# Counting a smaller, growing delay between last byte and use for the first twelve transfers, in the list that orders the first block

## The chip, the cores and the metric

The kernel runs on one core of one Trainium2 chip. The metric is the device time of one execution in microseconds (us); lower is better. The engines are called as in the profile: PE (TensorE matmuls), PEld (TensorE weight loads), DVE (VectorE), ACT (ScalarE), POOL (GpSimd), SP (SyncE, which here issues every DMA; SPq is its queue).

## What is computed

A windowed attention (4 batches, 8 heads, 576 positions, head width 64; heads 0 to 3 look back 32 positions, heads 4 to 7 look back 128 in steps of 4), then two feed-forward layers over 2304 tokens of width 512 with 2048 hidden units:

```python
scores = np.where(masks, scale * np.matmul(q, k.transpose(0, 1, 3, 2)), -1e9)
attn = softmax(scores)                      # rows
x = np.matmul(attn, v)                      # -> (2304, 512)
h = x @ w_in                                # layer 1, rational activation
P = a[0] + a[1] * h + a[2] * h**2 + a[3] * h**3
Q = 1.0 + np.abs(b[0]) * np.abs(h) + np.abs(b[1]) * h**2
x = (P / (Q + 1e-06)) @ w_out
h = x @ w2_in                               # layer 2, PReLU
out = (np.maximum(h, 0.0) + alpha * np.minimum(h, 0.0)) @ w2_out
```

The softmax is written out here as one call; the reference subtracts the row maximum, takes the exponential and divides by the sum plus 1e-9. All arrays are float32; the layer-1 weights come in as 64-bit words, from which a float32 is rebuilt on the chip (`w_convert`).

## The kernel before

The 2304 tokens are cut into six blocks of 384 (`BLK`). The attention of a block is four units U (pairs of heads); units 0 to 3 are block 0, units 4 to 7 block 1. One unit goes through these steps: its qk and v tiles are loaded (`u_load`, L439 and L441); PE writes the mask into PSUM (`put`, L458) and adds the scores on top (L478); DVE takes the row maxima `mx` (L492) and scales them to `nm` (L496); ACT takes the exponentials `p` with their sums `sm` (L512); DVE inverts the sums to `rd` (L522, L523), and either DVE (L541, units 0 to 3) or ACT (L532, later units) normalises `p`; PE transposes it (L549); ACT (L568) and DVE (L570) copy the transposes to `pts`; PE multiplies by v (L582, the "PV" below); ACT copies the result to `xh` (L609), and from block 1 on DVE takes the remainder `xl` (L615).

Layer 1 then runs in pairs of hidden chunks. For a chunk c ("item") PE does eight matmul instructions of `xh` with the rebuilt weights `win` (L645, two a matmul in block 0), into one of two PSUM banks `ps_h`; ACT makes `ta` (L663) and `tc` (L664) from it; DVE works on `tc` (L665, L666), and L666 is the last reader of the bank; the pair's rest (`rat_2`) alternates DVE L672, ACT L673 and L674, DVE L675 to L677. The second matmuls (L695, `outproj1`) accumulate into `ps_y`. The weights of a chunk pair are rebuilt by two ACT copies (L375, first `raw_inh`, then `raw_outh`) and DVE steps (L381, two L391, two L396). In the trace the first weight tiles are `win_342`, `win_418`, `wout_495` and `win_503`, in this order; the number is the tile's.

All loads go through SP's queue in the order of the string `ORDER` at the start: mask constants, qk of unit 0, identity, qk of unit 1, two small tables, v of unit 0, qk of unit 2, and so on, then weights. Ten `warm` matmuls (L963, 128x512 bf16) and 64 `fill` matmuls (L967, 128x256 bf16) compute nothing that is used.

The order of instructions on PE, DVE, ACT and SP is not the order in which the code writes them. `in_order_of_need` collects all instructions, derives which needs which, gives each a level (the longest chain behind it), and then runs a list schedule in an assumed time: on the engine that is free first it takes the instruction with the highest level among those that are ready within `SLACK` (100 ns). What starts before `ORDERED` (115 us of the assumed time) is fixed in this order on its engine; all the rest keeps the code's order behind it. Nothing is timed on the chip for this: costs come from `_cost`, and the landing of a transfer from these lines (L245 to L248):

```python
            parts, width = size[k]
            begin = max(start + 1600, landed)
            landed = begin + parts * width / (412 if parts == 128 else 210)
            done = landed + (2700 if begin > start + 1700 else 900)
```

So the list lets one transfer's bytes follow the other's at 412 bytes a ns, and counts another 900 ns (transfer alone) or 2700 ns (it had to queue behind an earlier one) from its last byte to the moment at which an engine may use it. The real semaphores decide on the chip; the list only decides who stands before whom on each engine, and an engine runs its instructions in that order.

Of the kernel before, what the change touches and what calls it, by code (L numbers as in the profile page):

```python
# [29 lines left out]
FILLS = (64,)  # L30
W_BIAS = 2.0 ** -112
NARROW = 2.1
SLACK = 100.0
FILL = 256
ORDERED = 115e3
# [65 lines left out]
def _cost(i):  # L101
# [22 lines left out]
    if e == mybir.EngineType.Activation:  # L124
        far = outs and any(abs(s) != 1 for s, _ in outs[0].ap[-1:]) and outs[0].dtype == F32R
        acc = len(outs) > 1
        occ = max(165, (1.7 if far else NARROW if outs[0].dtype == mybir.dt.uint16 else 0.95) * n) + 93 * pointers + 50 * acc
        return occ, occ + 145 + (12 if acc else 0)
# [7 lines left out]
def in_order_of_need(tc, nc, places):  # L136
# [88 lines left out]
            waiting[todo[k].engine].append(k)  # L225
    order = {e: [] for e in free}
    landed = 0.0
    for _ in range(n):
        pick = None
        for e, w in waiting.items():  # L230
            if not w:
                continue
            t = min(max(free[e], ready_at[k]) for k in w)
            if pick is None or t < pick[0]:
                pick = t, e
        t, e = pick
        limit = max(t, free[e]) + SLACK
        k = max((k for k in waiting[e] if ready_at[k] <= limit), key=lambda k: level[k])
        waiting[e].remove(k)
        start = max(free[e], ready_at[k])  # L240
        if start < ORDERED:
            order[e].append(k)
        free[e] = start + costs[k][0]
        if e == Engine.SP:
            parts, width = size[k]  # L245
            begin = max(start + 1600, landed)
            landed = begin + parts * width / (412 if parts == 128 else 210)
            done = landed + (2700 if begin > start + 1700 else 900)  # L248
        else:
            done = start + costs[k][1]  # L250
        for j, data in after[k]:
            left[j] -= 1
            ready_at[j] = max(ready_at[j], done if data else free[e])
            if not left[j]:
                waiting[todo[j].engine].append(j)
# [11 lines left out]
def attn_rational_prelu_kernel(  # L267
# [853 lines left out]
    rest()  # L1121
    out_some(len(todo))
    in_order_of_need(tc, nc, slots)


# [80 lines left out]
```

## Time and profile before

| what | value |
|---|---|
| time, median of 3 runs | 888.12 us (887.09, 888.12, 888.78) |
| the profiled execution: time, span | 887.51 us, 885.7 us |
| PE busy | 872.5 us, 99% of the span |
| DVE busy | 760.7 us, 86% |
| ACT busy | 613.3 us, 69% |
| DMA | 92.78 MB, mean 105 GB/s; 328 GB/s over the first 60 us |
| instructions | 14822 |

The profiled execution is one more run than the three. Its span runs from the first to the last recorded instruction; the 1.8 us by which its time is longer lie around it. Busy shares are means over stages; which engine holds up the end in a stage is read from a window or a chain of that stage.

### The profile page before, as it was taken

The numbers are of one execution on the slowest core, as the hardware profiler recorded it, in microseconds if no ns is written. First come the engines' busy times: TensorE is split into PE (matmuls) and PEld (weight loads), VectorE is DVE, ScalarE is ACT, GpSimd is POOL, SyncE is SP. The second block draws the span as 40 slices with busy tenths as digits, with TensorE's granted clock in tenths as the row PEclk, the third lists the DMA queues.
The fourth block names the chain that finished last, engine by engine and source line by source line (L and its number), as shares of the span: only waits on it lengthen the run. The fifth ranks groups of instructions, "written<-read, shape, count | busy, mean of one in ns | idle before, by whom it ended". The sixth has DMA issues, their size and how long they took to land.

```text
span 885.7 us, 14822 instructions
## 1 busy us (share of the span) xinstructions
PE 872.5 (99%) x5746; PEld 779.0 (88%) x5746; DVE 760.7 (86%) x1199; ACT 613.3 (69%) x1253; POOL 0.2 (0%) x4
## 2 busy tenths in 40 slices
PE   9999999999999999999999999999999999999997
PEld 6555678999999999999999999898888989899896
DVE  5999999999999998988899999998986778767652
ACT  6999988788877888887677576557554456635423
POOL 0000000000000000000000000000000000000000
PEclk9999999999999999999999999999999999999999
DMA  9964212133334434440021242323320011210001
GB/s 346 407 238 176 82 57 79 38 115 140 130 109 139 173 125 148 160 149 19 20 78 42 95 131 95 119 79 119 101 85 24 27 46 60 97 47 25 1 0 72
DMA packets 32903, 92.78 MB, mean 105 GB/s; under 512 B 3905, under 2 KB 11329, under 8 KB 32833
## 3 DMA queue, kind: packets, MB, share of 16 engines
q1 hardware_dynamic: 32832, 91.83, 29.9%
q8 instruction: 45, 0.74, 0.3%
q14 instruction: 26, 0.20, 0.1%
HBM read 76.61 MB, written 15.20 MB: 104 GB/s over the span
## 4 chain that ended last, share of the span: by engine, by line
PE 57%; ACT 18%; DVE 18%; DMA 4%; issue 2%; SPq 0%; ACTq 0%
PE ps_h L836 19%; PE ps_y L714 14%; PE ps_y L695 9%; PE ps_h L645 7%; PE ps_aS L714 4%; PE ps_aP L714 3%; ACT p L512 3%; DVE tb L675 2%; DVE tc L676 2%; ACT p L532 2%; ACT tc L664 2%; ACT ta L673 2%; DVE tc L677 2%; ACT ta L674 2%; ACT ta L663 1%
## 5 line engine op out<-in xcount | busy, mean ns | idle before, releaser
L645 PE MATMUL ps_h<-xh,winh 128*128 128x384 f32 x320 | 110.4, 345 | 2.7 <-DVE tc L666 2.2
L695 PE MATMUL ps_y<-gh,wouth 128*128 128x384 f32 x320 | 108.4, 339 | 0.0
L695 PE MATMUL ps_y<-gl,wouth 128*128 128x384 f32 x320 | 107.1, 335 | 0.3 <-DVE gl L685 0.3
L695 PE MATMUL ps_y<-gh,woutl 128*128 128x384 f32 x320 | 107.2, 335 | 0.0
L645 PE MATMUL ps_h<-xh,winl 128*128 128x384 f32 x320 | 107.2, 335 | 0.0
L645 PE MATMUL ps_h<-xl,winh 128*128 128x384 f32 x320 | 107.1, 335 | 0.0
L714 PE MATMUL ps_y<-wouth,gl 128*128 128x512 f32 x192 | 74.9, 390 | 0.0
L714 PE MATMUL ps_y<-woutl,gh 128*128 128x512 f32 x192 | 74.9, 390 | 0.0
L714 PE MATMUL ps_y<-wouth,gh 128*128 128x512 f32 x192 | 74.8, 390 | 0.0
L663 ACT ACTIVATE ta<-ps_h,root 128x384 f32<-128x384 f32 x96 | 57.3, 596 | 18.7 <-PE ps_h L645 18.4
L664 ACT ACTIVATE tc<-ps_h,co 128x384 f32<-128x384 f32 x96 | 66.5, 694 | 0.0
L645 PEld LDWEIGHTS ps_h<-xh,winh 128*128 128x128 f32 x320 | 60.0, 188 | 6.9 <-DVE tc L666 3.7
L742 ACT ACTIVATE gh<-tc 128x768 fp32r<-128x768 f32 x48 | 40.3, 841 | 30.5 <-PE ps_aP L714 28.0
L695 PEld LDWEIGHTS ps_y<-gl,wouth 128*128 128x128 f32 x320 | 60.2, 188 | 0.6 <-DVE gl L685 0.6
L645 PEld LDWEIGHTS ps_h<-xl,winh 128*128 128x128 f32 x320 | 60.1, 188 | 0.3
L743 DVE TENSOR_TENSOR gl<-tc,gh 128x768 fp32r<-128x768 f32 x48 | 45.8, 954 | 16.9 <-ACT gh L742 16.7
L695 PEld LDWEIGHTS ps_y<-gh,wouth 128*128 128x128 f32 x320 | 60.2, 188 | 0.0
L742 ACT ACTIVATE st_a<-w 128x1024 fp32r<-128x1024 f32 x24 | 25.5, 1061 | 50.1 <-PE ps_h L836 41.4
L695 PEld LDWEIGHTS ps_y<-gh,woutl 128*128 128x128 f32 x320 | 60.1, 188 | 0.0
L645 PEld LDWEIGHTS ps_h<-xh,winl 128*128 128x128 f32 x320 | 60.1, 188 | 0.0
L675 DVE SCALAR_TENSOR_TENSOR tb<-tb,ta 128x768 f32<-128x768 f32 x48 | 45.8, 955 | 16.3 <-ACT ta L674 16.0
L666 DVE SCALAR_TENSOR_TENSOR tc<-tc,co,ps_h 128x384 f32<-128x384 f32 x96 | 58.1, 608 | 0.7
(197 smaller groups left out, 2317.8 us busy)
## 6 DMA issues: line engine op xcount, KB each, us to landing
w<-w_dram_in SPq DMA_DIRECT2D x24, 512.0 KB, 3.6
raw<-in_w_in_dram SPq DMA_DIRECT2D x16, 512.0 KB, 5.1
raw_inh<-in_w_out_dram SPq DMA_DIRECT2D x13, 512.0 KB, 3.8
ld_qk<-in_qk_d_dram SPq DMA_DIRECT2D x12, 512.0 KB, 5.0
ld_v<-in_v_d_dram SPq DMA_DIRECT2D x12, 512.0 KB, 4.1
ld_qk<-in_qk_p_dram SPq DMA_DIRECT2D x12, 416.0 KB, 4.2
ld_v<-in_v_p_dram SPq DMA_DIRECT2D x12, 384.0 KB, 3.4
y_dram<-os SPq DMA_DIRECT2D x24, 192.0 KB, 1.9
```

The costliest lines, as they stand in the source:

```text
L512: nc.scalar.activation(out=a["p"][h][:m, t * n:(t + 1) * n], in_=a["s"][h][:m, t * n:(t + 1) * n], func=AF.Exp, scale=scale, bias=a["nm"][ ...
L532: nc.scalar.activation(out=pv, in_=pv, func=AF.Copy, scale=rd[:m, t:t + 1])
L645: nc.tensor.matmul(out=hp[:, :BLK], lhsT=w, rhs=x, start=(k == 0), stop=(k == len(pairs) - 1))
L663: nc.scalar.activation(out=ta, in_=hp, func=AF.Abs, scale=root)
L664: nc.scalar.activation(out=tc_, in_=hp, func=AF.Identity, scale=co[:, 3:4], bias=co[:, 2:3])
L666: nc.vector.scalar_tensor_tensor(out=tc_, in0=tc_, scalar=co[:, 1:2], in1=hp, op0=ALU.add, op1=ALU.mult)
L675: nc.vector.scalar_tensor_tensor(out=tb, in0=tb, scalar=C1, in1=ta, op0=ALU.add, op1=ALU.mult)
L695: nc.tensor.matmul(out=yt[:, :BLK], lhsT=w[:, m * 128:(m + 1) * 128], rhs=g, start=(c == 0 and i == 0), stop=(c == NC - 1 and i == len(pai ...
L714: nc.tensor.matmul(out=yt, lhsT=g[:, tok], rhs=w, start=(first and i == 0), stop=(last and i == 2))
L742: nc.scalar.activation(out=hi, in_=t, func=AF.Copy)
L743: nc.vector.tensor_tensor(out=lo, in0=t, in1=hi.bitcast(F32), op=ALU.subtract)
L836: nc.tensor.matmul(out=hp, lhsT=u[:, ws], rhs=x[:, xs], start=(k == 0), stop=(k == 5))
```

## The change

```diff
+LAG = 2700
...
     order = {e: [] for e in free}
     landed = 0.0
+    issued = []
...
             begin = max(start + 1600, landed)
             landed = begin + parts * width / (412 if parts == 128 else 210)
-            done = landed + (2700 if begin > start + 1700 else 900)
+            done = landed + (min(LAG, 300 + 450 * len(issued)) if begin > start + 1700 or len(issued) < 12 else 900)
+            issued.append(k)
```

The delay from last byte to use is now 300, 750, 1200, 1650, 2100 and 2550 ns for the first six transfers, then 2700 ns up to the twelfth whether they queue or not; from the thirteenth on it is as before (2700 for one that queued, 900 for one alone). Nothing is added to the program or taken from it: the instructions are the same, and only their order moves. The three new lines also move the line numbers: below L248 every line of the changed kernel is 3 higher (L512 is L515, L967 is L970).

In PE's order the start of the program changes. Of the rows of before, this is the piece from the end of unit 0's scores (`ps_y_251`, `ps_y_252`) to the first score of unit 1 (`ps_aS`); the pair of L967 rows stands 22 times there, and ten warm-ups stand before it:

```order
L478 MATMUL ps_y_252<-ld_qk 64x96
L458 LDWEIGHTS msk
L458 MATMUL ps_y_351<-msk 64x320
L967 LDWEIGHTS msk
L967 MATMUL ps_h<-msk 128x256
...
L478 MATMUL ps_aS<-ld_qk 64x96
```

The same place in the change, where seven warm-ups stand before the masks, two between masks and unit 0's scores, and one after these; the pair of L970 rows stands 12 times:

```order
L481 MATMUL ps_y_252<-ld_qk 64x96
L966 LDWEIGHTS warm
L966 MATMUL ps_h<-warm 128x512
L970 LDWEIGHTS msk
L970 MATMUL ps_h<-msk 128x256
...
L481 MATMUL ps_aS<-ld_qk 64x96
```

Ten fills that stood ahead of unit 1's scores now stand later: between the first two transposes and unit 2's scores, and around unit 3's.

On ACT the rows from the end of unit 0's part to the first weight copies, before:

```order
L988 ACTIVATE root<-root 128x1
L609 ACTIVATE xh_416<-ps_h 128x384
L512 ACTIVATE p,sm<-ps_y_350,nm 112x80 x4
L512 ACTIVATE p,sm<-ps_y_351,nm 112x80 x4
L512 ACTIVATE p,sm<-ps_y_426,nm 112x80 x4
L512 ACTIVATE p,sm<-ps_y_427,nm 112x80
L568 ACTIVATE pts<-ps_aS 96x384
L512 ACTIVATE p,sm<-ps_y_427,nm 112x80 x3
L375 ACTIVATE win_342<-raw_inh_150 128x512
```

and in the change:

```order
L991 ACTIVATE root<-root 128x1
L571 ACTIVATE pts<-ps_aS 96x384
L612 ACTIVATE xh_416<-ps_h 128x384
L515 ACTIVATE p,sm<-ps_y_350,nm 112x80 x4
L515 ACTIVATE p,sm<-ps_y_351,nm 112x80 x4
L515 ACTIVATE p,sm<-ps_y_426,nm 112x80 x4
L515 ACTIVATE p,sm<-ps_y_427,nm 112x80 x4
L378 ACTIVATE win_342<-raw_inh_150 128x512
```

The copy of unit 1's transposes (`pts<-ps_aS`) moved from the exponentials of unit 3 to before those of unit 2 (`ps_y_350`, `ps_y_351`).

Further on ACT, from the copies of `wout_495` over unit 4's exponentials (`ps_aS`, `ps_aP`) to the first rational steps, before:

```order
L375 ACTIVATE wout_495<-raw_inh_158 128x512
L375 ACTIVATE wout_495<-raw_outh_160 128x512
L609 ACTIVATE xh_580<-ps_h 128x2x4x48
L375 ACTIVATE win_503<-raw_inh_166 128x512
L512 ACTIVATE p,sm<-ps_aS,nm 128x96 x3
L512 ACTIVATE p,sm<-ps_aP,nm 128x96 x3
L663 ACTIVATE ta<-ps_h,root 128x384
L664 ACTIVATE tc<-ps_h,co 128x384
```

and in the change:

```order
L378 ACTIVATE wout_495<-raw_inh_158 128x512
L612 ACTIVATE xh_580<-ps_h 128x2x4x48
L378 ACTIVATE wout_495<-raw_outh_160 128x512
L666 ACTIVATE ta<-ps_h,root 128x384
L515 ACTIVATE p,sm<-ps_aS,nm 128x96 x3
L515 ACTIVATE p,sm<-ps_aP,nm 128x96 x3
L667 ACTIVATE tc<-ps_h,co 128x384
...
L676 ACTIVATE ta<-tb,c1t 128x768
L378 ACTIVATE win_503<-raw_inh_166 128x512
```

The first `ta` now stands ahead of unit 4's exponentials, and the copy of `win_503` moved from ahead of them to behind the first L676 (L673 before).

## Rows read from the trace of the kernel before

**Rows 1.** The page: its first line, and busy time (share of the span) of PE.

```profile
span 885.7 us, 14822 instructions
...
PE 872.5 (99%) x5746; PEld 779.0 (88%) x5746; DVE 760.7 (86%) x1199; ACT 613.3 (69%) x1253; POOL 0.2 (0%) x4
```

**Rows 2.** Windows: start:end, length, busy (x instructions) by engine, PEclk, DMA share, GB/s.

```profile
26.20:36.00 9.80, 8.17 (x55) 4.60 (x51) 9.39 (x20) 8.72 (x29) 0.00 (x0) 1.00 1.03 405
36.00:48.30 12.30, 11.67 (x57) 6.33 (x58) 11.70 (x22) 12.30 (x31) 0.00 (x0) 1.00 1.03 408
...
54.30:127.00 72.70, 72.08 (x463) 45.74 (x463) 71.78 (x118) 71.74 (x152) 0.00 (x0) 1.00 0.33 117
127.00:883.00 756.00, 750.73 (x4778) 701.46 (x4778) 646.15 (x987) 496.46 (x958) 0.00 (x0) 1.00 0.26 85
```

**Rows 3.** Timeline, first 9 us, PE and PEld: start, us, engine, line, out<-in, [idle before].

```profile
1.72 0.15 PEld L963 LDWEIGHTS <-warm 128*128 128x128 bf16 x1 [0.28 <-issue]
...
4.28 0.37 PEld L963 LDWEIGHTS <-warm 128*128 128x128 bf16 x2 [0.28 <-issue]
...
6.11 2.30 PEld L967 LDWEIGHTS <-msk 128*128 128x128 bf16 x22 [0.15 <-issue]
...
8.62 0.29 PE L478 MATMUL ps_aS<-ld_qk 64*64 64x96 f32 x1
```

**Rows 4.** Unit 1's qk: its issue (timeline of SP), and from the DMA view, us to landing.

```profile
2.11 0.43 SPq L439 DMA_DIRECT2D ld_qk<-in_qk_p_dram  x1
...
ld_qk<-in_qk_p_dram SPq DMA_DIRECT2D x1, 416.0 KB, 4.7
```

**Rows 5.** Timeline of DVE: scaled maxima of units 1 and 4, last reader of the second bank.

```profile
10.25 0.17 DVE L496 TENSOR_SCALAR nm<-mx 128x6 f32<-128x6 f32 x1
...
27.65 0.16 DVE L496 TENSOR_SCALAR nm<-mx 128x6 f32<-128x6 f32 x1
...
35.25 0.61 DVE L666 SCALAR_TENSOR_TENSOR tc<-tc,co,ps_h 128x384 f32<-128x384 f32 x1
```

**Rows 6.** Timeline of ACT, 10 to 50 us.

```profile
10.52 0.34 ACT L512 ACTIVATE p<-ps_aS,nm 128x96 f32<-128x96 f32 x1 [1.04 <-DVE ba L986]
...
14.68 0.33 ACT L512 ACTIVATE p<-ps_y,nm 112x80 f32<-112x80 f32 x1
...
18.81 0.49 ACT L568 ACTIVATE pts<-ps_aS 96x384 f32<-96x384 f32 x1
...
25.30 0.91 ACT L609 ACTIVATE xh<-ps_h 128x384 f32<-128x384 f32 x1
26.30 0.67 ACT L375 ACTIVATE win<-raw_inh 128x512 f32<-128x512 f32 x1
27.91 0.34 ACT L512 ACTIVATE p<-ps_aS,nm 128x96 f32<-128x96 f32 x1 [0.93 <-DVE nm L496]
...
29.82 0.61 ACT L663 ACTIVATE ta<-ps_h,root 128x384 f32<-128x384 f32 x1
...
35.72 0.84 ACT L674 ACTIVATE ta<-ta 128x768 f32<-128x768 f32 x1
...
47.81 1.72 ACT L532 ACTIVATE p<-p,rd 128x96 f32<-128x96 f32 x6
```

**Rows 7.** Timeline of PE, 24 to 49 us.

```profile
24.72 0.88 PE L645 MATMUL ps_h<-xh,win 128*128 128x384 f32 x2 [0.16 <-DVE win L396]
...
26.19 4.78 PE L645 MATMUL ps_h<-xh,win 128*128 128x384 f32 x14
...
35.92 2.20 PE L645 MATMUL ps_h<-xh,win 128*128 128x384 f32 x6 [0.64 <-DVE tc L666]
...
48.26 0.31 PE L549 MATMUL ps_aS<-ident,p 128*96 128x128 f32 x1 [0.30 <-ACT p L532]
```

**Rows 8.** Waits, 100 to 150 us, PE's own: in total, times, longest.

```profile
PE ps_h L582 <- ACT wouth L416: 0.4, 1, 0.4
...
PE ps_h L645 <- DVE tc L666: 0.2, 1, 0.2
```

## The prediction

> **What bounds the kernel now.** Start with the busy times. PE is busy 872.5 of 885.7 us [rows 1], so 13.2 us are all that any reordering could take away. The windows by stage say where they lie [rows 2]. From 127 to 883 us PE is busy 750.73 of 756.00: this lies behind nearly all that the list fixes, and PE sets its pace. From 54.3 to 127 PE, DVE and ACT are busy 72.08, 71.78 and 71.74 of 72.70: three engines are full at once, so a lead of one of them alone is worth nothing there. Only before 48.3 does PE stand still for long: 1.63 us between 26.2 and 36, 0.63 between 36 and 48.3, where ACT has none left (12.30 of 12.30). The question is thus how much earlier PE comes through the first 54 us, and whether ACT and DVE come along. The granted clock reads 1.00 in all these stretches.
>
> **The start.** The timeline shows the cost of a pessimistic list: between unit 0's scores and unit 1's stand 22 fills, 2.30 us, 0.105 us each, and unit 1's scores begin at 8.62 [rows 3]. Their qk was issued at 2.11 and landed 4.7 us later, at 6.8 [rows 4]. The old list adds 2700 ns to that transfer's last byte, the new one, for the fourth transfer, 300 + 3 x 450 = 1650; the difference, 1.05 us, is ten fills of 0.105. All else ahead of unit 1's scores is the same set of instructions in another order, so they begin at 8.62 - 1.05 = 7.6. That is still 0.8 after the landing: no wait takes the place of the fills. The ten fills return later, where PE waits for DVE and ACT anyway; if that cover were gone they would cost 1.05.
>
> On DVE unit 1's `nm` now stands directly behind the maxima instead of behind one small operation on `sm` (0.1 us). So it comes from 10.25 [rows 5] to about 9.1, and unit 1's exponentials come from 10.52 [rows 6] to 9.4: a lead of 1.1 to 1.2.
>
> Unit 2 keeps part of it. Its maxima now stand on DVE in front of the copy of `ps_aP`, but its `nm` behind that copy, which waits for unit 1's transposes; by the order of steps its exponentials start at about 14.3 instead of 14.68 [rows 6], 0.4 earlier. ACT's copy of `ps_aS` (0.49 with its tail, about 0.4 of ACT's time, at 18.81 before) is done ahead of them now, which brings the lead back to 0.7 or 0.8 when unit 3's exponentials end. From there to the first L645 the three orders are nearly alike, so I carry 0.7: PE's first matmul of item 0 starts at 24.0 instead of 24.72 [rows 7]. That it is not the full 1.05 is a choice between ends, 0.4 (what unit 2's start keeps) and 1.05 (unit 1's lead); the copy decides for the upper half.
>
> **What ACT gives back.** After the weights of `wout_495` the old order gives ACT the copy of `win_503` at 26.30, then unit 4's exponentials at 27.91, held 0.93 by DVE's `nm` at 27.65 [rows 5, 6]. The new order gives it `ta` of item 0 next. Item 0 needs eight of the sixteen L645 instructions, 4.78/14 = 0.34 each, with unit 4's scores between them (from 25.60, where the first two end, to 26.19 before) [rows 7]: 24.0 + 8 x 0.34 + 0.6 = 27.3 or 27.4. ACT is done with its part at about 25.3 (the L609 that began at 25.30 no longer stands last and all is 0.7 earlier), so it stands 2.1 us, against 9.80 - 8.72 = 1.08 before [rows 2]. DVE's `nm` of unit 4 now has two L391 in front instead of one; DVE's lead pays for that one and no more, so it lies at 27.7 to 28.0. Unit 4's exponentials then start at about 28.2, end 27.91 to 29.82 = 1.91 later, at 30.1 [rows 6], and the same steps as before up to L674, `win_503` among them, end at 36.6; before it was 35.72 + 0.84 = 36.56 with the tail. ACT's lead is gone: between 0.2 behind and 0.2 ahead.
>
> PE keeps its lead a little longer. DVE reaches L666 of item 1, the last reader of the second bank, without its short waits for ACT, at some 34.9 instead of 35.86 [rows 5], so item 2's matmuls start at 35.1 instead of 35.92 [rows 7], 0.8 ahead. But ACT is full from there on, with the same work to do, and unit 5's normalising steps (47.81 before [rows 6]) start when they did. PE already waited for them at 48.26, 0.30 [rows 7]; now it arrives 0.5 to 0.6 earlier, takes two instructions of L695 forward and then waits for ACT. So about 0.5 of the 0.7 is late next at unit 5's transposes, and 0.2 stays.
>
> **Behind 54 us.** The list swaps more rows up to 115 us of its time: layer-1 work of items 2 and 3 ahead of weight copies on ACT, six matmuls of a later chunk into the front of one PE stretch, transposes of one unit split over two places. No row prices these. A gain is bounded by the waits that PE has there, 0.4 + 0.2 [rows 8]; a loss by the nearest wait for a DVE reader, 0.64 [rows 7]. I take nothing, as all three engines are full on either side, and keep both ends. SP issues the same loads; three late ones change places.
>
> **Sum.** -0.7 at item 0, +0.5 at unit 5, 0 behind: -0.2 us, against the profiled execution's 887.51 (885.7 of span and 1.8 around it): 887.3. That execution lies 0.6 below the median 888.12, inside the spread of the three runs (1.7); a new median may fall in between, so I take 887.8 as the base and predict 887.6. Bounds of the sum: -0.7 - 0.6 = -1.3 and +0.3 + 0.6 = +0.9. About 0.2% (1.8 us) is what a measurement of this kernel can tell from no change: below 886.0 is faster, above 889.6 slower.
>
> **Rivals.**
> *The lead is kept and grows.* If ACT's standing at 25 to 27 is shorter than I reckon, item 2 and 3's steps, now ahead of weight copies, feed PE in time, and PE's idle time between 26.2 and 48.3 (2.26 us [rows 2]) shrinks as well. For it: the old list was wrong by 1 us just where PE did useless work. Against it: ACT is full from 36 us on. The lead alone gives 887.1, with all the idle time 884.8; the middle is 885.9. It decides if unit 5's normalising begins by 47.2.
>
> *ACT becomes late.* The copy of `win_503` moves from 26.30 to about 34.9. If ACT stands 2.1 instead of 1.08 and the lead doesn't cover it, that 1.07 shows at items 4 and 5, whose weights these are, and again at unit 5's transposes, 2.1 in all: 889.9, slower. For it: 36 to 48.3 has no idle ACT to absorb it. Against it: DVE's lead at L666. It decides once the first `win_503` copy starts after 35.9.
>
> *The clock rises later.* The loads of the warm-ups come every 0.43 us from 1.72 on and only the two at 4.28 within 0.37 together [rows 3], which is 512 columns at 1.2 and then 2.4 GHz. In the change sixteen short mask matmuls stand where the eighth warm-up did. If the lower level lasts over the twelve fills, they cost 12 x 0.105 = 1.26 more, unit 1 is 0.2 later than before, and what ACT loses (1.07 as above) is not covered: 1.3 later, 889.1. [...] PE has work without a break in both orders, so I give it little.
>
> *The change does nothing that counts*, since all that moves is hidden: 887.8, within the forecast.
>
> **How the numbers follow.** Forecast with "does nothing": 0.56, around 887.6, own range 886.5 to 888.7, the bounds of the sum. Lead kept 0.24; ACT late 0.14; clock 0.06. Faster: most of the second, 0.19, and 0.03 of the forecast's tail, 0.22. Slower: 0.10 of ACT late and 0.02 of tail, 0.12. Same: 0.66. The range 885.3 to 889.8 leaves out the lower part of "lead kept" (0.08) and the upper of "ACT late" (0.08).
>
> **What would show it.** Right, if the profile of the change has: twelve fills before unit 1's scores, which begin near 7.6; the first L645 near 24.0; ACT idle about 2 us before the first `ta`; item 2 near 35.1; unit 5's first transpose waiting for L532 at 48.3; equal times from there. Wrong, if L532 of unit 5 starts a microsecond earlier or later than 47.81, or if PE gets new waits between 54 and 130 us.

## The result: 892.3 us, slower by 0.5%

The change runs in 892.34 us (median of 11 runs, 890.43 to 896.96); the kernel before, beside it, in 887.70 (11 runs, 886.42 to 890.92). The ratio is 1.0052, with a 95% interval of 1.0038 to 1.0066. The prediction, 887.6 with 889.8 as its upper end, was wrong.

**The profile after.** The profiled execution took 891.03 us. From the page, its first line and the busy times, the lines that answer to [rows 1]:

```profile
span 889.3 us, 14819 instructions
...
PE 874.5 (98%) x5745; PEld 779.0 (88%) x5746; DVE 760.9 (86%) x1199; ACT 613.9 (69%) x1253; POOL 0.2 (0%) x4
```

The windows of [rows 2], with the same columns:

```profile
26.20:36.00 9.80, 7.86 (x67) 4.39 (x66) 9.35 (x19) 7.40 (x26) 0.00 (x0) 1.00 1.02 404
36.00:48.30 12.30, 11.87 (x71) 6.74 (x66) 10.34 (x19) 12.30 (x31) 0.00 (x0) 1.00 1.03 409
54.30:127.00 72.70, 71.47 (x417) 44.54 (x415) 71.87 (x118) 72.27 (x152) 0.00 (x0) 1.00 0.33 117
127.00:883.00 756.00, 751.78 (x4819) 701.78 (x4820) 647.98 (x989) 496.16 (x956) 0.00 (x0) 1.00 0.25 84
```

Between 26.2 and 36 ACT does 1.32 us less than before (7.40, not 8.72), and then it is full to 48.3; from 54.3 to 127 PE does 0.61 less.

The start, from the timelines of PE and of its weight loads, for [rows 3]:

```profile
4.41 0.51 PEld L461 LDWEIGHTS <-msk 64*64 64x64 bf16 x16 [0.84 <-issue]
5.31 0.13 PEld L966 LDWEIGHTS <-warm 128*128 128x128 bf16 x2 [0.38 <-issue]
...
6.18 0.73 PE L481 MATMUL ps_y<-ld_qk 64*64 64x96 f32 x24
7.07 1.47 PE L970 MATMUL ps_h<-msk 128*128 128x256 bf16 x12 [0.16 <-issue]
8.47 0.29 PE L481 MATMUL ps_aS<-ld_qk 64*64 64x96 f32 x1
```

Twelve fills stand there, as foretold. But unit 0's scores begin at 6.18, not at 5.36 as before:

```profile
5.36 0.70 PE L478 MATMUL ps_y<-ld_qk 64*64 64x96 f32 x21
```

So unit 1's begin at 8.47, a mere 0.15 earlier than 8.62.

DVE around unit 4's scaled maxima, for the second line of [rows 5]:

```profile
27.03 0.68 DVE L394 SCALAR_TENSOR_TENSOR win<-raw_inh,win 128x512 uint32<-128x512 uint32 x1
27.63 0.45 DVE L495 TENSOR_REDUCE mx<-ps_aS 128x3 f32<-128x288 f32 x1
...
28.36 0.68 DVE L394 SCALAR_TENSOR_TENSOR win<-raw_outh,win 128x512 uint32<-128x512 uint32 x1
28.96 0.17 DVE L499 TENSOR_SCALAR nm<-mx 128x6 f32<-128x6 f32 x1
```

ACT, for [rows 6]: exponentials of units 1 and 2, the last copy of `wout_495`, the first `ta`, unit 4's exponentials, the first copy of `win_503`, unit 5's normalising steps:

```profile
10.37 0.34 ACT L515 ACTIVATE p<-ps_aS,nm 128x96 f32<-128x96 f32 x1
...
15.41 0.32 ACT L515 ACTIVATE p<-ps_y,nm 112x80 f32<-112x80 f32 x1
...
25.71 0.67 ACT L378 ACTIVATE wout<-raw_outh 128x512 f32<-128x512 f32 x1
28.75 0.58 ACT L666 ACTIVATE ta<-ps_h,root 128x384 f32<-128x384 f32 x1 [2.36 <-PE ps_h L648]
29.22 0.34 ACT L515 ACTIVATE p<-ps_aS,nm 128x96 f32<-128x96 f32 x1
...
36.06 0.66 ACT L378 ACTIVATE win<-raw_inh 128x512 f32<-128x512 f32 x1
...
49.18 1.75 ACT L535 ACTIVATE p<-p,rd 128x96 f32<-128x96 f32 x6
```

And PE, for [rows 7]: item 0, unit 4's first score among it, unit 4's transposes, item 2, unit 5's transposes:

```profile
25.04 1.53 PE L648 MATMUL ps_h<-xh,win 128*128 128x384 f32 x4 [0.16 <-DVE win L399]
26.49 0.29 PE L481 MATMUL ps_aS<-ld_qk 64*64 64x96 f32 x1
...
33.18 0.84 PE L552 MATMUL ps_aS<-ident,p 128*96 128x128 f32 x3 [1.89 <-ACT p L535]
...
36.48 2.85 PE L648 MATMUL ps_h<-xh,win 128*128 128x384 f32 x8
...
49.67 0.57 PE L552 MATMUL ps_aS<-ident,p 128*96 128x128 f32 x2 [0.40 <-ACT p L535]
```

Four matmuls of item 0 stand ahead of unit 4's scores, not two; these come at 26.49 (25.53 before). DVE does a first weight step before the maxima can begin and a second ahead of `nm`, which comes at 28.96 (27.65 before). ACT meanwhile waits 2.36 us for `ps_h`, with `ta` first in its queue. Unit 4's exponentials start 1.31 later than before, and PE waits 1.89 for their end instead of 0.93. Unit 5's normalising steps are 1.37 late.

PE's waits between 54 and 200 us, for [rows 8]:

```profile
PE ps_h L648 <- DVE tc L669: 0.7, 1, 0.7
PE ps_h L585 <- DVE tc L669: 0.7, 1, 0.7
PE ps_h L585 <- issue: 0.4, 1, 0.4
PE ps_aS L552 <- ACT p L535: 0.2, 1, 0.2
```

Before there were three waits in this stretch, the two of [rows 8] and this one: 0.9 us then, 2.0 now.

```profile
PE ps_y L695 <- DVE gl L685: 0.3, 1, 0.3
```

### The profile page after: what moved, and what is told of

Its sections match the earlier page's. It is cut to its first block, busy times and chain, and to the rows that moved or that the text cites. A ratio compares the mean times of both kernels' runs of the same rounds, so it can differ in the third digit from the quotient of the medians.

```text
span 889.3 us, 14819 instructions
## 1 busy us (share of the span) xinstructions
PE 874.5 (98%) x5745; PEld 779.0 (88%) x5746; DVE 760.9 (86%) x1199; ACT 613.9 (69%) x1253; POOL 0.2 (0%) x4
## 4 chain that ended last, share of the span: by engine, by line
PE 56%; DVE 21%; ACT 19%; issue 2%; DMA 1%; SPq 0%; ACTq 0%
PE ps_h L839 19%; PE ps_y L717 14%; PE ps_y L698 7%; PE ps_h L648 6%; PE ps_aS L717 4%; PE ps_aP L717 3%; ACT p L515 3%; DVE tc L679 3%; DVE tb L678 3%; ACT p L535 2%; ACT ta L676 2%; DVE tc L680 2%; ACT tc L667 2%; ACT ta L677 2%; ACT ta L666 2%
## 5 line engine op out<-in xcount | busy, mean ns | idle before, releaser
L717 PE MATMUL ps_y<-wouth,gh 128*128 128x512 f32 x192 | 74.8, 390 | 0.0
L745 ACT ACTIVATE st_a<-w 128x1024 fp32r<-128x1024 f32 x24 | 25.5, 1062 | 50.1 <-PE ps_h L839 41.4
```

The costliest lines, as they stand in the source:

```text
L717: nc.tensor.matmul(out=yt, lhsT=g[:, tok], rhs=w, start=(first and i == 0), stop=(last and i == 2))
L745: nc.scalar.activation(out=hi, in_=t, func=AF.Copy)
```

## The experiments

In most kernels the list is worked out twice, with the old delays (0) and the new (1), and every engine's order is put together from pieces of the two, cut by the old list's times in ns. Each piece holds whatever the old list starts in it. The core, as a diff against the kernel before (the first four kernels write the same with two pieces, `head` and `tail`):

```diff
+    lists = listed(False), listed(True)
+    at = {k: start for ks in lists[0].values() for k, start in ks}
+    order = {e: [] for e in lists[0]}
+    low = -1
+    for which, high in PIECES:
+        for e in order:
+            order[e] += [k for k, start in lists[which][e] if low <= at[k] < high and start < ORDERED]
+        low = high
```

Line numbers in these kernels are 8 to 25 higher than in the kernel before.

**Four cuts: the start, and 50 us.** The first has the new order only up to unit 0's scores, the second only behind them; the third up to 50 us, the fourth only behind it.

```diff
# e1_start_new
+CUT = 5340.0
+    head, tail = (new, old)
# e2_start_old
+CUT = 5340.0
+    head, tail = (old, new)
# e3_new_to_50
+CUT = 50e3
+    head, tail = (new, old)
# e4_old_to_50
+CUT = 50e3
+    head, tail = (old, new)
```

> Only the first 26 matmuls and unit 0's scores (what the old list starts before 5.34 us) stand in the new order, that is seven warm-ups, sixteen masks, two warm-ups, the scores, one warm-up; all behind is in the old order. Clock theory (the masks among the warm-ups let the array's lower level last longer): unit 0's scores begin at about 6.2 instead of 5.36, the 22 fills follow, unit 1's scores at about 9.4, and the time is 0.5 to 1 us above 887.7. Order theory (the clock has no part; what costs is the order behind the start): scores of unit 0 near 5.2, time 887.7 within 0.5.

> The complement: start in the old order (ten warm-ups, masks, unit 0's scores), all behind in the new order. Clock theory: unit 0's scores at 5.36 and unit 1's near 7.6, the first L645 near 24.0, and most of the 4.6 us of the change comes back: 887.5 to 889. Order theory: unit 1 is early as well, but unit 4's exponentials still wait behind the first ta and the swaps behind 54 us still cost, so the time stays at 890.5 to 892.5.

> New order for all that the old list starts before 50 us, old order behind it. If the loss comes from the first 50 us alone and the rest of it grows out of PE being 1 us late in a stage where three engines are full: 891 to 892. If the new order behind 50 us has its own price: PE is 1.0 late at 54 us as in the change, and the time is 888.5 to 889.

> Old order before 50 us, new order behind. If the loss comes from the first 50 us: 887.7 within 0.5. If the new order behind 50 us has its own price: everything is as before up to 54 us, and the time is 2 to 3 us above, 890 to 891.

Measured: e1 0.9997 (0.9987 to 1.0008), e2 1.0036 (1.0022 to 1.0049), e3 1.0026 (1.0012 to 1.0040), e4 1.0011 (0.9998 to 1.0024). The start alone costs nothing, though unit 5's first PV product is 0.68 us late in its profile (55.14, not 54.46). The stretch from 5 to 50 us costs most; of the order behind 50 us the interval allows nothing to 2 us.

Times counted from a profile's start carry chance. Unit 0's scores begin at 5.28 to 6.03 us in the eleven profiles of this document whose start has the old order, and at 5.53 to 6.28 in the nine with the new one (means 5.66 and 6.07). The profile before, with 5.36, is an early one. What is late by half a us in one profile is compared more safely from one event of a profile to another of the same profile.

**Finer pieces.** New between 5.3 and 25.5 us, new between 25.5 and 50, all new but that stretch, new between 50 and 85.

```diff
# e5_new_5_25
+PIECES = ((0, 5340), (1, 25500), (0, 1e9))
# e6_new_25_50
+PIECES = ((0, 25500), (1, 50e3), (0, 1e9))
# e7_old_25_50
+PIECES = ((1, 25500), (0, 50e3), (1, 1e9))
# e8_new_50_85
+PIECES = ((0, 50e3), (1, 85e3), (0, 1e9))
```

> The old order up to 5.3 us of the old list's times and from 25.5 us on; between them the new one: twelve fills ahead of unit 1's scores, unit 2's nm behind the copy. Theory A (what is lost lies in ACT's order from 25 to 50 us): the lead of unit 1's scores, 0.7 us in the run with the old start, is gone when item 0 begins, near 24.7, and nothing is late behind it: 888.3 to 888.8 beside 888.6, ratio 0.9997 to 1.0003, unit 5's normalising steps at 47.8 to 48.0. Theory B (unit 2's nm behind the copy is what costs, since DVE and ACT are late from there on): ratio 1.002 to 1.003, normalising steps after 48.8. If the lead is kept it is faster, 0.999.

> Only the stretch from 25.5 to 50 us of the old list's times in the new order: ACT's first ta of item 0 stands ahead of unit 4's exponentials, and the first copy of win_503 behind ta of item 1's second half. Theory A: all of the middle's loss is here; unit 4's exponentials start 1.0 to 1.3 later than 27.91, unit 5's normalising steps at 48.8 to 49.2, ratio 1.0020 to 1.0028 (1.8 to 2.5 us). Theory B: nothing is late, ratio 1.000 to 1.0007, normalising steps at 47.8 to 48.1.

> The whole of the new order but for the stretch from 25.5 to 50 us, which has the old one. Theory A: only the tail's loss is left, 1.0 us as in the run with the old order up to 50 us: ratio 1.0008 to 1.0015, unit 5's normalising steps at 48.1 to 48.4. Theory B: as the whole change, 1.003 to 1.005. If the loss in the middle and the one of the tail aren't a sum, it may come out below 1.0008.

> The old order up to 50 us of the old list's times and behind 85; between them the new one: a unit's transposes split by output matmuls, masks in another order, DVE's steps of layer 1 shuffled against each other. If the tail's 1.0 us comes from these rows (theory C), ratio 1.0008 to 1.0015, with PE waits for DVE near 103 and 126 us, and first stores of a block 1 to 1.5 later than 135.8, 215.9, 294.6. If it comes from the rows behind 85 (theory D), ratio 0.9995 to 1.0005 and none of these.

Measured: e5 1.0028 (1.0010 to 1.0046), e6 1.0019 (1.0006 to 1.0032), e7 1.0038 (1.0021 to 1.0055), e8 0.9994 (0.9982 to 1.0006). Neither theory holds by itself. With theory A, e7 should have come to 1.0015 at most; with theory B, e6 should have been nothing. Two profiles, of e6 and e7, showed one reason why the parts need not add up: the granted clock reads 0.50, the 1.2 GHz level, for some seven us behind PE's wait at unit 4's transposes. The profiles of before and of the change showed nothing of the kind.

**ACT's rows alone, the order behind 85 us, and a cover for the wait.** f1 moves eleven rows of ACT and nothing on other engines; f2 takes ACT's rows back in the change; f3 is new behind 85 us only; f4 is the change with twelve small matmuls in PE's wait.

```diff
# f1_act_alone (the pieces hold for ACT; 0 on the other engines)
+PIECES = ((0, 25500), (1, 36000), (0, 1e9))
...
# f2_act_back (the pieces hold for ACT; 1 on the other engines)
+PIECES = ((1, 25500), (0, 36000), (1, 1e9))
...
# f3_new_behind_85
+PIECES = ((0, 85e3), (1, 1e9))
# f4_cover (other lines set these matmuls directly ahead of unit 4's transposes in PE's order)
...
+            if not J:
+                cover = bank("y0")
+                for _ in range(12):
+                    nc.tensor.matmul(out=cover[:, :COVER], lhsT=ident16, rhs=msk[:, :COVER], start=True, stop=True)
```

> The kernel before with eleven rows of ACT alone in the new order (25.5 to 36 us of the old list's times): first ta ahead of unit 4's exponentials, the first copy of win_503 behind the last of them; PE, DVE and SP keep the old order row by row. Theory A (this order is the middle's loss): unit 4's exponentials start 1.0 to 1.5 later than 27.91, PE waits 1.5 to 1.9 ahead of unit 4's transposes, unit 5's normalising steps at 48.6 to 49.2; ratio 1.0018 to 1.0026, as the run with this stretch new on all engines. Rival (the loss came from PE's and DVE's rows of that stretch): ratio within 1.0005 of 1.

> The changed kernel with these rows of ACT alone (25.5 to 36 us) back in the old order. Theory A: the middle's loss of about 2 us goes, what is left is that of the other stretches, 1.0 to 1.6: ratio 1.0012 to 1.0030 instead of 1.0052, unit 5's normalising steps a microsecond earlier than 49.18. Rival: 1.0045 to 1.0055 as the whole change.

> The old order up to 85 us of the old list's times, the new one behind. The new order behind 50 us cost 1.0, the piece from 50 to 85 alone gained 0.5 or nothing; so by a sum this one costs 1.0 to 1.5: ratio 1.0010 to 1.0018, with a PE wait for a DVE reader near 180 us where the change splits the transposes. Rival (the losses don't add up, the runs' spread is the difference): 0.9995 to 1.0007.

> The changed kernel with twelve small matmuls of the mask table (128x255, about 0.106 us each, 1.3 us in all, into a bank that is free) directly ahead of unit 4's transposes, where PE stands 1.9 us; all other rows are those of the change. If PE's standing there is what lets the granted clock fall for some microseconds in a part of the runs (theory E): at most 2 of 12 runs show a mean clock below 0.998, against 7 of 11 of the change, and the median is 890.4 to 891.2, ratio about 1.003 to 1.004. If the standing has nothing to do with it: as many low clocks as before and 892.0 to 892.6. If the matmuls are in the way, 1 us more than the change.

Measured: f1 1.0016 (1.0004 to 1.0029), f2 1.0067 (1.0049 to 1.0085), f3 0.9998 (0.9987 to 1.0009), f4 1.0028 (1.0018 to 1.0037). In f1's timeline of ACT, unit 4's exponentials wait behind `ta`, though DVE had their `nm` ready at 28.0:

```profile
28.62 0.58 ACT L680 ACTIVATE ta<-ps_h,root 128x384 f32<-128x384 f32 x1 [2.21 <-PE ps_h L662]
29.10 0.33 ACT L529 ACTIVATE p<-ps_aS,nm 128x96 f32<-128x96 f32 x1
```

In f2's they are first in the queue and wait as long for DVE:

```profile
29.39 0.34 ACT L529 ACTIVATE p<-ps_aS,nm 128x96 f32<-128x96 f32 x1 [1.93 <-DVE nm L513]
```

So there are two paths to unit 4's exponentials, and the change makes both late (29.10 and 29.39 here, 27.91 before); giving back one of them gains nothing. Theory A falls as it stood: ACT's rows alone are enough to cost 1.4 us (0.0016 x 888.4), the clock's part included, but in the change DVE's lateness hides them.

f4 shows the clock's part. PE's timeline, with the small matmuls and what is left of the wait, and the windows behind it (the granted clock is the third number from the end):

```profile
31.61 1.47 PE L1068 MATMUL ps_y<-msk 128*128 128x255 bf16 x12
33.67 0.84 PE L560 MATMUL ps_aS<-ident,p 128*96 128x128 f32 x3 [0.59 <-ACT p L543]
```

```profile
34.00:36.00 2.00, 1.95 (x12) 0.97 (x14) 2.00 (x5) 1.96 (x7) 0.00 (x0) 1.00 1.04 409
36.00:38.00 2.00, 2.00 (x30) 1.46 (x30) 0.66 (x2) 2.00 (x4) 0.00 (x0) 1.00 1.01 405
```

Windows of f2's profile, whose PE waits 1.82 (to 33.26):

```profile
32.00:34.00 2.00, 0.74 (x3) 0.40 (x3) 1.94 (x5) 2.00 (x7) 0.00 (x0) 0.94 1.04 414
34.00:36.00 2.00, 2.00 (x12) 1.15 (x13) 0.52 (x1) 1.82 (x6) 0.00 (x0) 0.50 1.03 404
...
38.00:40.00 2.00, 2.00 (x4) 1.09 (x5) 1.82 (x3) 2.00 (x4) 0.00 (x0) 0.50 1.03 412
40.00:42.00 2.00, 2.00 (x19) 1.03 (x18) 2.00 (x4) 0.79 (x2) 0.00 (x0) 0.85 1.02 408
```

PE is busy 0.74 of the two us from 32 to 34; then its clock falls to 1.2 GHz for some seven us. Each run lists the mean clock of its span. Of the change's 11 runs seven show under 0.998, with a median of 892.42; the other four have 890.89. Of f4's 12 runs none does, and the median is 890.92. The cover gives back 1.4 us by these medians, 2.1 by the ratios (1.0028 and 1.0052, each to the kernel before that ran beside it), and the intervals of the two ratios, 1.0018 to 1.0037 and 1.0038 to 1.0066, don't overlap.

**The cover elsewhere, and unit 4's chain given back whole.** g1 is the kernel before with seven small matmuls, g2 is e8 with seven, g3 is f1 with twelve; g4 is the change with 22 to 36 us old on all engines.

```diff
# g1_before_cover, g2_e8_cover (as f4_cover, on before and on e8)
+                for _ in range(7):
# g3_act_alone_cover (as f4_cover, on f1)
+                for _ in range(12):
# g4_unit4_old
+PIECES = ((1, 22e3), (0, 36e3), (1, 1e9))
```

> The kernel before with seven small matmuls of the mask table (0.75 us in all) directly ahead of unit 4's transposes, where its PE stands 0.93. Theory E (this standing lets the granted clock fall in a part of the runs): no run under 0.998, where 3 of 29 and 4 of 30 of the kernel before were; the median falls by 0.2 to 0.6 since the slowest runs go, ratio 0.9990 to 1.0000. Rival: the low clocks of the kernel before come from elsewhere, nothing changes.

> The new order between 50 and 85 us alone, as before, and the seven small matmuls ahead of unit 4's transposes. The new piece alone gave 0.9994 (interval 0.9982 to 1.0006); with the cover 0.9980 to 0.9996. If that piece was nothing but spread, the same time as the kernel before with the cover.

> The kernel before with the eleven rows of ACT in the new order, and twelve small matmuls ahead of unit 4's transposes. It tells the two parts of that run's 1.2 us apart. Theory E: no run under 0.998 (7 of 12 without the matmuls), ratio 1.0006 to 1.0013: the lateness of unit 4 alone, 0.5 to 1.2 us. If the clock has no part: 1.0016 as without them, as many low clocks.

> The changed kernel with the stretch from 22 to 36 us old on every engine: unit 4's scores behind two matmuls of item 0 and not four, its nm behind one weight step and not two, its exponentials ahead of ta. Theory F (each of these alone is enough to make unit 4 1.2 to 1.3 us late, so giving back ACT's rows alone gained nothing): unit 4's exponentials start at 28.1 to 28.6 instead of 29.22, PE waits 0.9 to 1.2 ahead of its transposes instead of 1.89, at most 4 of 12 runs under 0.998, ratio 1.0010 to 1.0025 instead of 1.0052. Rival: the loss lies in the start or the tail; 1.004 to 1.005.

Measured: g1 1.0009 (1.0000 to 1.0018), g2 1.0001 (0.9992 to 1.0011), g3 1.0016 (1.0007 to 1.0024), g4 1.0032 (1.0020 to 1.0044). The cover is no gain where the wait is 0.93. In g3 it takes low clocks from 7 of 12 to 3 of 11 but gives no time, where theory E expected 1.0013 at most. These three can't tell what the cover is worth at unit 4, though. Between the block stores at 373 and at 447 us the profiles of g1, g2 and g3 spend 75.1 to 75.7 us, those of before, e8 and f1 74.0 to 74.3, so a gain may be lost there. f4's comparison is free of that: the change spends 75.40 there, f4 75.63. In g3's profile, where the clock doesn't fall, unit 5's first PV product begins 46.75 us behind unit 1's first score (45.84 before), in f1's, with 3.4 us at the lower level, 47.47. So 0.9 us is lateness; how much of the other 0.7 f1's executions pay on average isn't known. (In f2's profile the clock was low for 6.8 us.) Nothing beats the kernel before.

g4 does what it should at unit 4: exponentials at 27.59, earlier than before's 27.91, PE's wait 0.93, no run of 6 under 0.998. And still it loses. Its timeline of ACT, at items 2 and 3:

```profile
39.15 0.58 ACT L679 ACTIVATE ta<-ps_h,root 128x384 f32<-128x384 f32 x1 [0.65 <-PE ps_h L661]
...
42.39 0.58 ACT L679 ACTIVATE ta<-ps_h,root 128x384 f32<-128x384 f32 x1 [0.42 <-PE ps_h L661]
...
45.64 0.35 ACT L528 ACTIVATE p<-ps_aS,nm 128x96 f32<-128x96 f32 x1
```

The new order puts `ta` ahead of weight copies here as well. ACT stands 0.65 and 0.42, and unit 5's exponentials are 0.98 late (45.64, not 44.66): what unit 4 won is lost 10 us on. The larger part of g4's loss comes later still: from unit 0's first score to unit 5's first PV product it takes 49.49 us (49.10 before), from there to the first block's stores 82.64 (81.35 before).

**The same with 22 to 50 us old, and only the part ahead of 22 us new.**

```diff
# h1_new_22_old_50
+PIECES = ((1, 22e3), (0, 50e3), (1, 1e9))
# h2_new_to_22
+PIECES = ((1, 22e3), (0, 1e9))
```

> The changed kernel with the whole stretch from 22 to 50 us old on every engine: besides unit 4's chain, ACT's ta of items 2 and 3 is behind the weight copies again, where ACT stood 0.65 and 0.42 us in the run with 22 to 36 us old. Theory G (ta ahead of work that is ready makes ACT stand, at item 0 and again at items 2 and 3, and ACT has no room up to 48 us): unit 5's normalising steps start at 47.3 to 48.0 instead of 48.78, ratio 1.0000 to 1.0012, what is left being the order behind 50 us. Rival: it stays at 1.003, and the loss is in the order behind 50 us.

> The new order up to 22 us of the old list's times (the start, the ten fewer fills ahead of unit 1's scores, the attention steps of units 1 to 3), the old one from there on: what the smaller delays were for, alone. Theory G: item 0 begins 0.1 to 0.5 earlier than 24.72, unit 5's normalising steps at 47.3 to 47.9, and the end moves by a part of that: ratio 0.9992 to 1.0002. Rival (the attention steps' order is itself late): 1.001 to 1.0025, with unit 4's exponentials after 28.3.

Measured: h1 1.0031 (1.0020 to 1.0042), h2 1.0006 (0.9996 to 1.0016). In h1 unit 5's normalising steps start at 48.28 (49.18 in the change, 47.81 before), a little outside what theory G expected; its profile is one that starts late, with unit 0's scores at 6.27. The time doesn't come down to what G expected. In h1's profile the lag grows from 0.49 us at unit 5's PV products (54.95) to 1.4 at the first block's stores (137.2, not 135.8) and 2.7 at 450, as it does in the change. So the rival is the nearer one. The order behind 50 us costs h1 no more than e4: from unit 5's first PV product to the first block's stores h1 takes 82.28 and e4 82.37. What h1 has on top is the stretch from the stores at 373 to those at 447: 75.16 us, 73.92 in e4.

h2 says that the part the new delays are about gains nothing that stands out of the noise. Its profile is a poor witness. Unit 1's scores come 0.57 earlier (8.05) and item 0 0.84 later (25.56), because PE stands 0.89 us at 16 us, in the middle of fills, and the profile shows nothing that it waits for. h1 has the same rows on PE, DVE and ACT up to 48 us and no such wait: its item 0 begins 16.55 us behind unit 1's first score, h2's 17.51. (e6's profile has such a wait too, 0.75.)

## Why the prediction was wrong

Two terms of the sum failed, and one was missing. "0 behind" was the largest error: behind unit 5's first PV product the profile of the change is 2.6 us slower (by place; 1.1 of it seem to go with the order ahead of 22 us, see below). "-0.7 at item 0" was -0.5 counted from unit 0's first score, and unit 4's `nm` came 1.0 us or more later than foretold. That PE's longer wait behind it would cost clock as well stood in no term.

**Where the 4.6 us are.** 1.4 to 2.1 are the clock behind unit 4's wait: shown by f4. The profiled execution, whose clock did not fall, is 3.6 longer in span. (Together that is more than 4.6: the pieces below hold some chance of this pair of executions, the first above all.) These lines, before and after in turn, divide it into stretches: unit 5's first PV product, and the stores at 136, 373 and 447 us, the first of which are the first block's.

```profile
54.46 0.92 PE L582 MATMUL ps_h<-pts,ld_v 96*64 96x64 f32 x24
55.44 0.92 PE L585 MATMUL ps_h<-pts,ld_v 96*64 96x64 f32 x24
...
135.81 4.13 SPq L702 DMA_DIRECT2D y_dram<-os  x4
138.21 4.25 SPq L705 DMA_DIRECT2D y_dram<-os  x4
...
372.97 4.90 SPq L702 DMA_DIRECT2D y_dram<-os  x4
375.54 6.01 SPq L705 DMA_DIRECT2D y_dram<-os  x4
...
447.23 4.43 SPq L702 DMA_DIRECT2D y_dram<-os  x4
450.94 4.43 SPq L705 DMA_DIRECT2D y_dram<-os  x4
```

```
stretch, us                           before  change   more
start to unit 0's first score           5.36    6.18   0.82
to unit 5's first PV product           49.10   49.26   0.16
to the first block's stores            81.35   82.77   1.42
to the stores at 373                  237.16  237.33   0.17
to the stores at 447                   74.26   75.40   1.14
to the end                            438.47  438.36  -0.11
```

The first piece is in part the chance of this pair, and e1, which has this start, costs nothing. The second says that, without the clock's part, the order ahead of 54 us neither wins nor loses much there. The third is the order behind 50 us, with the new waits of PE: this stretch takes 82.28 to 82.77 us in all eight profiles with that order (change, e2, e4, e7, f2, f4, g4, h1) and 81.33 to 81.84 in the other twelve. e4, which has two of the waits (0.39 at 102.6, 0.64 at 126.0), is 1.0 us slower with an interval that touches zero. Neither part of that order does it by itself: 81.41 in e8 (50 to 85 us), 81.54 in f3 (behind 85). Which rows do it wasn't found.

The 1.14 between 373 and 447 us isn't the change's alone: g1, which differs from the kernel before by seven small matmuls 340 us earlier, has the same two waits. PE's timeline of g1:

```profile
386.03 0.44 PE L653 MATMUL ps_h<-xh,winh 128*128 128x384 f32 x1 [0.31 <-DVE xl L623]
393.61 0.44 PE L653 MATMUL ps_h<-xh,winh 128*128 128x384 f32 x1 [1.04 <-DVE tc L674]
```

where the kernel before has one of 0.81, at 392.33. Between the stores at 373 and at 447 us seven of the 20 profiles spend about 74 us, two 74.6 and 74.8, and eleven 75.1 to 75.7. The seven (before, e1, e4, e6, e8, f1, f3) have the old order from 5 to 22 us and no small matmuls at unit 4; each of the thirteen has the new order there, or the small matmuls. What ties this to a stretch 340 us later stays open, and with it 1 us of the account.

**Step by step.**
- *"All else ahead of unit 1's scores is the same set of instructions in another order, so they begin at 8.62 - 1.05 = 7.6."* Ten fills less were worth 0.97 (8.47 - 6.18 = 2.29 between the two units' scores, 3.26 before). But unit 0's scores came 0.82 later: the two warm-ups ahead of them took 0.43 each, the rate of the lower clock. The rival on the clock was right on this, and wrong on its price: e1, which has this start alone, costs nothing. How late it is differs between executions: in g4's profile, with the same rows up to there, unit 1's scores begin at 7.82.
- *"Its exponentials start at about 14.3 instead of 14.68."* They start at 15.41, that is 6.94 behind unit 1's first score, where 6.7 was foretold and 6.06 stood before; in e2, where unit 1 leads by 0.68, still at 15.06. With `nm` behind the copy of `ps_aP`, unit 2 hangs on unit 1's transposes, and most of the lead ends there. Item 0 began at 25.04, not at 24.0; 0.87 of that is already there at unit 1's scores (8.47, not 7.6). From unit 0's first score to item 0 the change takes 18.86, before 19.36: a lead of 0.5, which the late start hid.
- *"DVE's lead pays for that one and no more, so it lies at 27.7 to 28.0."* This step failed, and it brought the clock's part with it. `nm` came at 28.96, 1.31 later than before: 0.32 was there at item 0, 0.64 came from PE's scores (1.45 behind item 0's start, 0.81 before), 0.35 from DVE's weight steps (2.47 from the scores to `nm`, 2.12 before). I read ACT's and DVE's orders here but not PE's, where unit 4's scores had moved behind four matmuls of item 0. ACT's standing was foretold well (2.1; measured 2.36), but "ACT's lead is gone: between 0.2 behind and 0.2 ahead" became 1.3 behind.
- *"I take nothing, as all three engines are full on either side."* This term was the furthest off: 1.42 up to the first block's stores, with 1.1 us more of waits on PE, and 1.14 between 373 and 447, where no row had been looked at. That three engines are full bounds what a lead can win; it was no reason for a price of nothing.
- *"The granted clock reads 1.00 in all these stretches"* was true of one execution. Of 145 runs of the kernel before, 19 have a mean under 0.998.
- The rival *ACT becomes late* had the place, the sign and the test right (the first copy of `win_503` starts at 36.06, behind the 35.9 from which it was to decide). Its price, 2.1 us, is near what e3 and e6 lose, but that is partly luck: their losses hold the clock's part, which it didn't price, and of the change's own profile only 0.16 is left of it at unit 5's PV products. I gave it 0.14, since I believed in a lead that wasn't there.

**What to carry over.** When a list is made anew, every engine's row for one chain has to be read, also where that chain begins: a late score on PE made DVE's and ACT's rows late whatever stood in them. A step that must wait, put ahead of steps that are ready, costs on an engine without room up to the next place where it is waited for; and two late paths to the same step hide each other, so taking back one shows nothing. Judge a wait of PE by several executions, not by one profile, since its price includes the clock behind it. Compare two profiles stretch by stretch, from event to event, since their starts differ by chance. And where no row prices what moves, a term of nothing needs a reason of its own.

## What was unexpected of the hardware

Behind a wait of PE of less than two us, in a stretch that is otherwise busy, the granted clock falls from 2.4 to 1.2 GHz in some executions of a program and not in others. Over all series, by PE's wait ahead of unit 4's transposes in the kernel's profile:

```
wait, us      kernels                                    runs  mean clock under 0.998
0.17          g1 g2                                        22     1
0.57 to 0.59  f4 g3                                        23     3
0.93 to 0.95  before (five series), e1 e4 e8 f3 g4 h1 h2  221    30
1.32 to 1.35  e5 e7                                        20     8
1.82 to 1.89  change, e2 e3 e6 f1 f2                       64    33
```

f2's profile, with 6.8 us at the lower level, is listed with a mean of 0.995. Only for profiled executions is it known that the fall lies there; of the others only the mean is listed. The count also misses short falls. f3's profile has one of 3.4 us, behind waits of 0.93 and 0.63, and is listed with 0.998:

```profile
36.00:38.00 2.00, 1.41 (x2) 0.84 (x3) 1.83 (x3) 2.00 (x5) 0.00 (x0) 0.64 1.03 412
38.00:40.00 2.00, 2.00 (x5) 1.01 (x3) 2.00 (x4) 2.00 (x5) 0.00 (x0) 0.51 1.02 408
```

It also gives the price. Up to 85 us of the list f3 has the rows of the kernel before; from unit 0's first score to unit 5's first PV product it takes 50.62 us, 49.10 before: 1.5 us for a fall of 3.4.

The Trainium skill (TensorE: Matmul & The Clock Gate, Part 1: The HAM clock gate) says that idleness brings the lower level back, and that the window in which the chip judges this runs freely and doesn't start anew with the kernel. The share of runs that grows with the wait agrees with both; no run here shows the second by itself.
